# A retention layer and a gated feed-forward on one core: another order of the seven second-layer products, and all first-layer weights through one load queue

## The chip, the core and the metric

The kernel runs on one core of a Trainium2 chip. The metric is the device time of one execution in microseconds (us). Kernels of one experiment call run on the same chip beside the kernel before. Times quoted are medians with the lowest and highest of their runs. A run more than 1.5% above the fastest of its kernel counts as slow, the others as fast. A ratio is the mean time of one kernel's fast runs over the mean of the other's fast runs of the same rounds, so it is not quite the ratio of the medians; its 95% interval follows in brackets. "Faster" or "slower" is said from 2% on.

Five engines work side by side: TensorE (PE in the profile; PEld are its weight loads), VectorE (DVE), ScalarE (ACT), GpSimd (POOL) and SyncE (SP), which here only starts loads and stores. PSUM is the memory that TensorE writes, in banks; SBUF is the working memory.

## The reference, cut to what matters

```python
scores = (q @ k^T) / 8                         # 8 batches x 8 heads, 576 positions, 64 columns
ret = scores * Dmat                            # gamma_h ** (i - j) for j <= i, else 0
x = (ret @ v) as 4608 tokens x 512
h = x @ w_in                                   # 512 -> 2048, the "first layer"
out = (h * cos(h)) @ w_out                     # 2048 -> 512, the "second layer"
```

## The kernel before

The retention is done chunk by chunk with a carried state. I call one chunk's group of small matmuls a *session*: it reads scaled and transposed Q and K tiles and scaled V, masks on VectorE, and leaves output (`xt`) that ScalarE copies for the first layer. The first layer works in *units* of four 128x512 matmuls (or eight of 256 columns): TensorE writes a PSUM bank, ScalarE makes the cosine (`cb`), VectorE multiplies bank and cosine into `gt` (0.69 us each), and only then is the bank free. W_in comes in eight *slabs* of 256 hidden units, float32 in memory, bfloat16 for TensorE.

The second layer of all blocks of 512 tokens but the first uses a seven-product scheme. Each product has two halves of eight 128x256 matmuls (0.87 us). What a product reads decides when it can start:

```python
left = {1: lambda: ((self.S1, HF * HB, 0, HB), [("s1", f) for f in range(HF)]),
        2: lambda: ((self.S5, HF * TB, HB, TB), s5), 3: lambda: of_gt(0, 0), 4: lambda: of_gt(1, 1),
        5: lambda: ((self.S5, HF * TB, 0, TB), s5), 6: lambda: of_gt(0, 1), 7: lambda: of_gt(1, 0)}
```

`of_gt(0, .)` is the lower half of the hidden units, `of_gt(1, .)` the upper half, `S5` and `S1` are sums of `gt` tiles made on VectorE (the *token sums*, four rounds for each block). The order and what follows each product:

```python
seq = ((4, "e", True, p4), (2, "e", False, p2), (3, "f", True, p3), (5, "f", False, p5),
       (1, "a", True, p1), (7, "a", False, p7), (6, "b", True, p6))
if last:
    seq = tuple(seq[i] for i in (0, 2, 4, 1, 3, 5))
```

and their weaving with the next block's units, in which `run` also spreads the sessions evenly:

```python
fs = [f for u in range(HF) for f in (u, u + HF)]        # units 0, 8, 1, 9, ...
for i, f in enumerate(fs[:0 if last else None]):
    ...                                                 # one first-layer unit
    mlp += two[i:i + 1]                                 # one half of a product
    if i in AT:
        mlp.append(lambda u=AT.index(i), j=j: self.token_sums(j + 1, u))
run(mlp, att_of(need[j + 1], need[j + 2]) if j + 2 < NTB else [])
```

This weaving is only the order in which work is handed to a scheduler inside the kernel's builder. It simulates the engines with estimated costs and decides the final order on each engine.

## Time and profile before

| | before |
|---|---|
| three runs before the prediction | 304.32, 304.94, 749.91 us |
| span of the profiled execution | 301.2 us |
| TensorE busy, granted clock | 95%, full speed in every slice |
| session that reads the third V tile (V2) starts | 39.05 us |
| from there to the start of the last matmul | 259.32 us |
| from there to the end | 2.79 us |

The page gives busy shares, the chain that ended last and groups of instructions. A timeline line is: start in us, length in us, engine, source line, operation, output<-input tiles, tile shapes, type, count, and in brackets the idle time before the group with what ended it. The shown end of a matmul lies about 0.17 us after the moment at which the next may start. I measured waits as the distance between the starts of neighbouring matmuls minus the usual distance of such a pair. Where records were missing I lined the trace up with the program's order and took their time out.

### The profile page before, as it was taken

Reading aid. Unit: us, or ns where it says so; the run is one execution under the profiler, and the core shown is the slowest. Engines: PE = TensorE matmul, PEld = TensorE weight load, DVE = VectorE, ACT = ScalarE, POOL = GpSimd, SP = SyncE. Lnnn points to the kernel's source line nnn. Section 1 sums busy time; section 2 is a strip of 40 time slices with the busy share of each in tenths; the row PEclk is TensorE's granted clock in tenths of the full one; section 3 lists DMA queues with packets and bytes.
Section 4 is the critical chain, followed back from the end, with each engine's and each line's share of the span. In section 5 each row is a group of like instructions: output and inputs, shape, how many; then the busy total and the mean of one; then the engine's idle time right before and its main releaser. Section 6 shows DMA issues by size and latency. Waiting matters only on the chain.

```text
span 301.2 us, 8764 instructions
## 1 busy us (share of the span) xinstructions
PE 286.9 (95%) x3637; PEld 204.0 (68%) x3673; DVE 241.0 (80%) x403; ACT 185.8 (62%) x320; POOL 145.1 (48%) x145
## 2 busy tenths in 40 slices
PE   8988999999999999998999899999999999999996
PEld 3467578865788885666667576666666667566585
DVE  5888999999898599789767976898689568847941
ACT  4076567846676567765776568766777676545421
POOL 4715762688555687279217930993140013003213
PEclk9999999999999999999999999999999999999999
DMA  8999999999999999999899946996302020211114
GB/s 205 301 288 278 247 198 217 195 241 215 160 250 227 191 258 226 201 192 193 182 219 226 196 98 155 234 205 143 92 33 74 1 66 6 72 35 37 35 37 139
DMA packets 124438, 49.45 MB, mean 164 GB/s; under 512 B 83952, under 2 KB 123888, under 8 KB 124400
## 3 DMA queue, kind: packets, MB, share of 16 engines
q1 hardware_dynamic: 121232, 45.76, 71.6%
q0 software_dynamic: 3168, 3.15, 6.4%
q8 instruction: 29, 0.48, 0.7%
q14 instruction: 9, 0.07, 0.1%
HBM read 36.70 MB, written 9.44 MB: 153 GB/s over the span
## 4 chain that ended last, share of the span: by engine, by line
PE 78%; DVE 10%; DMA 4%; issue 4%; SPq 3%; ACT 1%; DVEq 0%
PE bk L807 35%; PE bk L924 30%; PE bk L832 5%; DMA stg<-in_v_dram 4%; DVE gt L818 4%; PE st L638 2%; PE bk L617 1%; DVE gt L893 1%; PE bk L608 1%; SPq L424 1%; DVE os L959 1%; PE bk L627 1%; DVE nat L485 1%; SPq L457 1%; DVE s L886 1%
## 5 line engine op out<-in xcount | busy, mean ns | idle before, releaser
L807 PE MATMUL bk<-xt,win 128*128 128x512 bf16 (+2 forms) x781 | 135.5, 316 | 4.3 <-DVE gt L818 1.0
L815 ACT ACTIVATE cb<-bk,cpi 128x512 bf16<-128x512 f32 x144 | 98.4, 687 | 57.9 <-PE bk L807 53.6
L818 DVE TENSOR_TENSOR gt<-bk,cb 128x512 bf16<-128x512 f32 x144 | 97.5, 686 | 38.6 <-ACT cb L815 33.7
L807 PEld LDWEIGHTS bk<-xt,win 128*128 128x128 bf16 x808 | 72.1, 98 | 38.4 <-ACT xt L674 1.3
L959 POOL TENSOR_TENSOR sv<-sv,os 128x512 f32<-128x512 f32 x16 | 22.3, 1391 | 81.7 <-ACT os L968 43.1
L530 POOL TENSOR_TENSOR qnat<-qstg,wt 128x512 bf16<-128x512 f32 x36 | 39.9, 1128 | 17.1 <-DMA qstg<-in_q_dram 17.1
L674 ACT ACTIVATE sbd<-st 64x512 bf16<-64x512 f32 (+1 forms) x68 | 38.0, 559 | 12.6 <-PE bk L608 11.0
L674 ACT ACTIVATE xt<-bk 128x256 bf16<-128x256 f32 (+1 forms) x64 | 27.6, 489 | 19.1 <-PE bk L727 15.1
L520 POOL TENSOR_TENSOR nat<-stg,wt 128x512 bf16<-128x512 f32 x28 | 36.0, 1285 | 5.0 <-DMA stg<-in_v_dram 4.9
L924 PE MATMUL bk<-wout,gt 128*128 128x256 bf16 x256 | 31.6, 273 | 3.0 <-DVE gt L818 3.0
L485 POOL CAST nat<-stg 128x512 bf16<-128x512 f32 x36 | 26.6, 747 | 13.5 <-DMA stg<-in_k_dram 13.5
L924 PE MATMUL bk<-tw,gt 128*128 128x256 bf16 x256 | 32.6, 273 | 0.0
L924 PE MATMUL bk<-wout,s 128*128 128x256 bf16 x256 | 31.8, 273 | 0.0
L924 PEld LDWEIGHTS bk<-wout,gt 128*128 128x128 bf16 x256 | 24.2, 98 | 10.9 <-DVE gt L818 5.8
L886 DVE TENSOR_TENSOR s<-gt 128x1024 bf16<-128x1024 bf16 x32 | 28.3, 904 | 3.1 <-PE bk L924 3.0
L924 PEld LDWEIGHTS bk<-tw,gt 128*128 128x128 bf16 x256 | 24.5, 98 | 7.4 <-ACT sv L963 0.6
L893 DVE TENSOR_TENSOR gt<-gt 128x1024 bf16<-128x1024 bf16 x32 | 29.1, 910 | 0.0
L924 PEld LDWEIGHTS bk<-wout,s 128*128 128x128 bf16 x256 | 24.3, 98 | 6.6 <-DVE gt L818 0.4
L959 POOL TENSOR_TENSOR sv<-sv 128x512 f32<-128x512 f32 x8 | 10.8, 1355 | 23.1 <-ACT sv L963 20.1
L653 DVE TENSOR_TENSOR pt<-bk,tri 128x512 bf16<-128x512 f32 (+3 forms) x37 | 20.3, 565 | 1.5 <-PE bk L608 1.3
L890 DVE TENSOR_TENSOR s<-gt 128x512 bf16<-128x512 bf16 x32 | 18.6, 582 | 0.1
L959 DVE TENSOR_TENSOR os<-bk,sv 128x512 f32<-128x512 f32 (+1 forms) x17 | 10.8, 647 | 7.0 <-POOL sv L959 6.6
(72 smaller groups left out, 258.6 us busy)
## 6 DMA issues: line engine op xcount, KB each, us to landing
out_dram<-os SPq DMA_DIRECT2D x31, 256.0 KB, 3.5
qstg<-in_q_dram SPq DMA_DIRECT2D x12, 512.0 KB, 5.8
stg<-in_k_dram SPq DMA_DIRECT2D x24, 256.0 KB, 4.3
stg<-in_v_dram SPq DMA_DIRECT2D x24, 256.0 KB, 5.1
stg<-in_k_dram SPq DMA_DIRECT2D x4, 512.0 KB, 8.9
stg<-in_v_dram SPq DMA_DIRECT2D x4, 512.0 KB, 9.3
wout<-in_moe_w_out_dram POOLq DMA_DIRECT2D x4, 512.0 KB, 12.5
qstg<-in_q_dram SPq DMA_DIRECT2D x4, 384.0 KB, 7.0
```

The costliest lines, as they stand in the source:

```text
L485: self.P.add(eng, lambda e: e.tensor_copy(dst, src), r=r, w=w, cost=cost, port=eng == "pool")
L520: self.P.add(eng, lambda e: e.tensor_tensor(ap(self.NAT[na], 2 * DM, 0, 128, DM, [D, H], [1, D]), ap(self.STG[st], 2 * DM, 0, 128, DM, [D, ...
L530: self.P.add(eng, lambda e, x=x: e.tensor_tensor(ap(self.QNAT[slot], 2 * DM, 0, 128, x * DM, [D, H], [1, D]), ap(self.QSTG[slot], 2 * DM, ...
L653: inst = e.tensor_tensor(ap(pt, 1024, p0, n, 256 * x, [256, m], [64, 4], [1, 64]), ap(self.BK, NB * 512, p0, n, (lo, hi)[x] * 512 + 256, [ ...
L674: self.P.add(eng, (lambda e: e.activation(*io(), AF.Copy)) if eng == "act" else (lambda e: e.tensor_copy(*io())), r=r, w=w, cost=0.127 + 0 ...
L807: inst = e.matmul(self.bk(box.i, 0, 128, i * n, n), ap(self.WIN, 4 * DFF, 0, 128, c * DFF + 128 * f, [1, 128]), ap(self.XT, 4 * XR, 0, 128 ...
L815: self.P.add("act", lambda e: e.activation(ap(cb, TB, 0, 128, 0, [1, m]), self.bk(box.i, 0, 128, 0, m), AF.Sin, bias=self.CPI.ap(), scale= ...
L818: self.P.add("dve", lambda e: e.tensor_tensor(ap(gt, NF * TB, 0, 128, f0 * TB + lo - TB * j, [TB, len(fs)], [1, n]), self.half_bank(box.i, ...
L886: self.P.add("dve", lambda e: e.tensor_tensor(ap(self.S5, HF * TB, 0, 128, f * TB, [1, 2 * TB]), ap(gt, NF * TB, 0, 128, f * TB, [1, 2 * TB]),
L893: self.P.add("dve", lambda e: e.tensor_tensor(ap(gt, NF * TB, 0, 128, f * TB + HB, [HF * TB - HB, 2], [TB, 2], [1, HB]), ap(gt, NF * TB, 0 ...
L924: inst = e.matmul(self.bk(box.i, 0, 128, at * HB, HB), ap(lt, lsize, 0, 128, loff + f * lstep + 128 * t, [1, 128]), ap(rt, rsize, 0, 128, ...
L959: self.P.add(eng, lambda e: e.tensor_tensor(out(), a(), b(), op), r=r, w=w, cost=1.04 if eng == "pool" else 0.09 + 0.00104 * n * HB, port= ...
```

## The change

The intent is threefold: get the V tiles sooner by putting all slabs on one queue behind K2; take the wait before each block's first product away by starting with product 3, which reads only lower units that are ready early when units run in rising order; and hold the last product back so that TensorE has something to do behind the last unit.

```diff
-AT = (9, 10, 12, 15)
+HOLD = (2, 4)
+LS = (0, 1, 2, 3, 4, 5)
+AT = (9, 11, 13, 15)
-EO, ES, EQ = ('act', 'act'), ('dve', 'act'), ('pool', 'pool')
-WP = (5, 5, 6, 8, 7, 8, 10, 1)
-WC = ("dve", "act", "act", "dve", "pool", "dve", "act", "dve")
-G1, G2, WG = 5, 5, ("stg", 1, 1, 0)
-EARLY = 8
-SOFT = (2, 6)
+EO, ES, EQ = ('act', 'act'), ('dve', 'dve'), ('pool', 'dve')
+WP = (7, 7, 7, 7, 8, 7, 7, 10)
+WC = ("dve", "act", "act", "dve", "pool", "dve", "dve", "act")
+G1, G2, WG = 3, 5, ("stg", 1, 1, 0)
+EARLY = 12
+SOFT = ()
-SHIFT = ('dve', 'dve')
-UNITS = ((0, 256, (0, 10)), (256, 512, (0, 10)), (0, 512, (10, 16)))
+SHIFT = ('act', 'dve')
+UNITS = ((0, 256, (0, 12)), (256, 512, (0, 12)), (0, 512, (12, 16)))
...
-        seq = ((4, "e", True, p4), (2, "e", False, p2), (3, "f", True, p3), (5, "f", False, p5),
+        seq = ((3, "f", True, p3), (4, "e", True, p4), (2, "e", False, p2), (5, "f", False, p5),
                (1, "a", True, p1), (7, "a", False, p7), (6, "b", True, p6))
         if last:
-            seq = tuple(seq[i] for i in (0, 2, 4, 1, 3, 5))
+            seq = tuple(seq[i] for i in LS)
...
-        BYPE, LEAD = 13, 2
+        BYPE, LEAD = 14, 2
...  (two cost estimates of the scheduler: a slab load 1.45 to 1.55, a product 0.9% more)
...  (K transposes copied by ScalarE instead of VectorE, in two places)
-                    self.step_tk(t, "dve")
+                    self.step_tk(t, "act")
...
-            for i, f in enumerate(fs[:0 if last else None]):
+            for f in range(0 if last else NF):
...
-                mlp += two[i:i + 1]
-                if i in AT:
+                mlp += two[f:min(f + 1, 14 - HOLD[j + 2 == NTB])]
+                if f in AT:
...
+            mlp += two[14 - HOLD[j + 2 == NTB]:14 if not last else 0]
```

`SOFT = (2, 6)` sent slabs 2, 3, 6 and 7 by two loads of GpSimd's queue that wrote bfloat16 directly; without it all eight slabs are cast by an engine. `BYPE` is the first group whose Q and K are turned by DMA instead of TensorE. I call the constants of the first group together with the K copies and `BYPE` the *start part*, the rest the *boundary part*.

More of the change, by code (lines that the diff above doesn't have):

```diff
@@ L459, in load_win @@
             bass.AP(self.w_in, s * 256, [[DFF, 128], [128 * DFF, 4], [1, 256]])),
-            w=keys, sem=f"wi{s}", cost=0.62, ring=1.45, pkt=0.04)
+            w=keys, sem=f"wi{s}", cost=0.62, ring=1.55, pkt=0.04)
     def load_soft(self, s, gate):
@@ L929, in mm @@
             return inst
-        self.P.add("pe", mm, r=lk + rk, w=[box], cost=HF * HB * 0.000422)
+        self.P.add("pe", mm, r=lk + rk, w=[box], cost=HF * HB * 0.000427)
     def bank(self, box, n=2):
@@ L976, in summed, with p3, p4 @@
             self.store(TB * j + HB * h + 128 * t, n, HB * c, HB, o)
-        def p4():
-            save("e", 0)
+        def p3():
+            save("f", 0)
         def p2():
             plain("e", 1, 0)
-        def p3():
-            add("dve", lambda: sv[0], lambda: self.bank(box["f"]), lambda: sv[0], ALU.add,
-                [box["f"], ("sv", 0)], [("sv", 0)])
+        def p4():
+            add("dve", lambda: sv[0], lambda: self.bank(box["e"]), lambda: sv[0], ALU.add,
+                [box["e"], ("sv", 0)], [("sv", 0)])
         def p5():
@@ L1119, in schedule @@
             for t in self.twos(tiles[g]):
-                self.step_tk(t, "dve")
+                self.step_tk(t, "act")
             for k in quads[g]:
@@ L1137, in schedule @@
         run([m1(lo, hi, *fs) for lo, hi, fs in units[EARLY:]], [lambda: T(need[0])] + att_of(need[0], req(640)))
-        fs = [f for u in range(HF) for f in (u, u + HF)]
         sums = [x for y in zip(self.weight_sums(0), self.weight_sums(1)) for x in y]
@@ L1151, in schedule @@
             mlp = two if last else []
-            for i, f in enumerate(fs[:0 if last else None]):
+            for f in range(0 if last else NF):
                 if j > 1:
                     mlp.append(m1(TB * (j + 1), TB * (j + 2), f))
-                elif i % 2 == 0:
-                    mlp.append(m1(1280, 1536, *(f // 2 * 2 + i % 4 // 2 * HF + x for x in range(2))))
-                mlp += two[i:i + 1]
-                if i in AT:
-                    mlp.append(lambda u=AT.index(i), j=j: self.token_sums(j + 1, u))
+                elif f % 2 == 0:
+                    mlp.append(m1(1280, 1536, f, f + 1))
+                mlp += two[f:min(f + 1, 14 - HOLD[j + 2 == NTB])]
+                if f in AT:
+                    mlp.append(lambda u=AT.index(f), j=j: self.token_sums(j + 1, u))
+            mlp += two[14 - HOLD[j + 2 == NTB]:14 if not last else 0]
             run(mlp, att_of(need[j + 1], need[j + 2]) if j + 2 < NTB else [])
```

## The prediction

> **What bounds the kernel now.** I read the busy summary and the forty slices first, then the TensorE timeline for every idle stretch, then the chain of waits for the start and the timeline for the tail.
>
> ```profile
> PE 286.9 (95%) x3637; PEld 204.0 (68%) x3673; DVE 241.0 (80%) x403; ACT 185.8 (62%) x320; POOL 145.1 (48%) x145
> ...
> PE   8988999999999999998999899999999999999996
> ...
> PEclk9999999999999999999999999999999999999999
> ```
>
> TensorE (PE) is busy nearly everywhere at the full clock. I check that by its pace, because the shown end of a matmul lies about 0.17 us behind the moment at which the next can start (four 128x512 matmuls are shown as 1.03 us long, yet the next group starts 0.87 us later). A first-layer unit (four 128x512 matmuls) takes 0.864 us of pace, half a second-layer product (eight 128x256) 0.87 us. That makes 144 units x 0.864 = 124.4, 112 halves x 0.87 = 97.4 and 64 plain second-layer matmuls x 0.216 = 13.8, together 235.6 us. None of it changes. So time can only come from TensorE's waits, from the start before it has steady work, and from the tail.
>
> ```profile
> 37.35 1.02 PE L807 MATMUL bk<-xt,win 128*128 128x512 bf16 x4 [0.46 <-DVE gt L818]
> 39.05 0.44 PE L721 MATMUL st<-sv,nat 64*64 64x64 bf16 x16 [0.68 <-DVE pt L698]
> ...
> 113.57 2.54 PE L807 MATMUL bk<-xt,win 128*128 128x512 bf16 x11 [0.55 <-ACT xt L674]
> ...
> 139.89 1.92 PE L924 MATMUL bk<-wout,gt 128*128 128x256 bf16 x16 [0.69 <-DVE gt L818]
> ...
> 170.71 1.92 PE L924 MATMUL bk<-wout,gt 128*128 128x256 bf16 x16 [1.23 <-DVE gt L818]
> ...
> 200.64 1.05 PE L924 MATMUL bk<-wout,gt 128*128 128x256 bf16 x8 [0.39 <-DVE gt L818]
> ...
> 286.25 3.67 PE L924 MATMUL bk<-wout,gt 128*128 128x256 bf16 x32 [0.71 <-DVE gt L818]
> ```
>
> The bracket is the idle time before the group and what ended it. These seven are all the real ones after 26.2 us; the many brackets of 0.16 beside groups of 3 or 11 are matmul records missing from the trace. With the 0.17 us added back they are worth 0.62, 0.84, 0.71, 0.86, 1.39, 0.55 and 0.88 us, 5.85 us in all. The last four are one event: a block's first product, number 4, reads the upper hidden units and waits until the last first-layer unit has gone through ScalarE (0.69 us) and VectorE (0.69 us).
>
> ```profile
> 9.34 11.38 DMA stg<-in_v_dram
> 20.74 1.29 DVE sv L509 x2
> 23.52 1.30 DVE gt L818 x2
> 26.30 5.39 PE bk L807 x48
> ```
>
> This is the start of the chain of waits. The second V load is issued at 9.3 us and lands at 20.7, because two W_in slabs on the same queue and two more through GpSimd's queue go before or beside it. TensorE is saturated only from 26.2 us.
>
> **What the Trainium skill says.** "Perfetto Trace Analysis", section Identifying the Most-Contended Engine, says that matmul busy share is a poor measure because matmuls are pipelined; the trace agrees (1.03 us shown, 0.87 us of pace), hence the count by pace. "DMA: Bandwidth & Descriptors", section Issuing engines are not separate DMA queues, says that DMAs started by different engines interleave on the same 16 DMA engines. The trace agrees: from 12.14 to 20.72 us two slabs (1.51 us each), one V load (1.8 us) and a 1 MB load of GpSimd's queue land, the last taking the remaining 3.8 us. So moving those slabs to the other queue makes no bandwidth; it only lets me choose the order. "SBUF — State Buffer", section Who interferes with whom, says that a VectorE instruction with two SBUF inputs contends with a GpSimd one that reads SBUF. The trace fits: the token sums (128x1024) average 904 ns, and 0.68 us at the end where GpSimd is idle.
>
> **The change, part by part.**
>
> *Start, worth about -1.85 us.* All eight slabs now go through the sync queue, behind K0 Q0 V0 K1 Q1 V1 K2. With the measured paces in the trace (K, Q or V 1.8 us, slab 1.51 us, Q1 at 12.14) I get: V1 13.95 (was 20.72), K2 15.75 (22.54), slab 0 17.3 (13.65), slabs 1, 2, 3, 5, 6 at 18.8, 20.3, 21.8, 23.3, 24.8, Q2 26.6 (25.82), slab 4 28.1, V2 29.9 (31.65), K3 31.7, slab 7 33.2, Q3 35.0, V3 36.8 (37.65). The bytes are the same, so the end of the loads hardly moves; V comes sooner, the first slab later.
> I then followed the order of instructions in the built program with durations from the trace. VectorE paces the stretch from 14 to 25 us: it has half of the Q scaling (0.7 us), V scaling 2 x 0.69, state copies 2 x 0.41, the Q transpose's copy 0.69, slab 0's cast 0.68, four masks 2.5 us. First first-layer unit: 19.95 us (was 17.6). Third big session: its mask at 21.1. Slab 1, cast on ScalarE (1.06 us) and then a table load (1.28 us), feeds the second unit at 21.95; slab 2's cast ends at 22.95 and feeds the third. Fourth session from about 23.95, then the steady stream from about 25.0 with three 256-column units done, against 26.24 with four: 1.24 - 0.87 = 0.37 us gained. From there the transpose copies (13 x 0.41 us) and half of the shifts (8 x 0.36 us) are off VectorE, which was 96 to 100% busy from 30 to 70 us, so I expect the two waits at 37.35 and 39.05 to go: 1.46 us. The session that started at 39.05 should start at about 37.2; equal TensorE work lies before it in both programs.
>
> *Block boundaries, -3.7 us.* Product 3 reads only the lower hidden units, early in the rising order, and its 1.75 us cover the last unit's way through ScalarE and VectorE before product 4. Two halves of product 6 (1.74 us) are held back behind the last unit as well. Three boundary waits go: 0.86 + 1.39 + 0.55. The 0.71 at 113.57 (a session's output was not yet copied) goes too, since the built program has five halves of products (4.4 us) after that session instead of two; with some 0.2 us of small waits near 177 to 200 us that is 3.7.
>
> *Last block, about 0.* The 0.88 at 286.25 goes by the same means (four halves held, 3.5 us). But the order is now 3, 4, 2, ..., and product 2 needs all token sums. Between the last unit's end and product 2 TensorE has 3.5 + 3.5 = 7.0 us of work. VectorE has about 1.7 us until that unit's output, then two output sums (2 x 0.68), two full rounds of token sums (2 x 1.74) and two of the third (1.06): 7.6, partly waiting for products. I expect a new wait of 0.9 us there, which eats the gain.
>
> *Tail, +0.45 us.*
>
> ```profile
> 295.86 1.27 POOL L959 TENSOR_TENSOR sv<-sv,os 128x512 f32<-128x512 f32 x1 [0.41 <-ACT os L968]
> 297.22 1.02 DVE L959 TENSOR_TENSOR os<-bk,sv 128x512 f32<-128x512 f32 x2 [6.58 <-POOL sv L959]
> ...
> 298.68 0.42 DVE L959 TENSOR_TENSOR os<-bk,sv 128x256 f32<-128x256 f32 x1 [0.44 <-PE bk L924]
> ```
>
> The GpSimd chain of the last block ends 1.5 us before TensorE does. Product 1 moves from third to fifth place, so its save (0.6) and two GpSimd sums (2 x 1.27) start only 3.5 us before TensorE's end and finish at about that end; then come two VectorE sums (2 x 0.42) where one came before.
>
> *Elsewhere, +1.2 us.* One more K and one more Q tile are transposed on TensorE (4 + 8 matmuls of 56 ns): +0.67. For new small waits I allow 0.5, since product 3's PSUM bank is now held across products 4 and 2.
>
> Sum: -1.85 - 3.7 + 0 + 0.45 + 1.2 = -3.9 us.
>
> **Rivals.**
> (a) The start gives more. If VectorE's queue does not hold up the first units (slab 0 is there at 17.3), the stream starts up to 2.5 us sooner: about 298 us. Against it: every VectorE item of that stretch stands in program order before slab 0's cast.
> (b) The start gives nothing or loses. W_in now arrives later than V; if a slab is late (slab 4, behind Q2 and cast by GpSimd, or slab 7), TensorE stalls between 29 and 36 us for 1 to 2 us: about 302.5. For it: my slack at slab 4 is only 2 us.
> (c) PSUM banks become the bound. Products 3/5 and 4/2 hold two of six banks together where one was held, and a session needs two. A wait of 0.4 us in each of seven blocks would take 2.8 us back: about 303. Against it: with products between them, units come only every 1.74 us and hold a bank about 2.7 us.
> (d) The gain is hidden by something already there, such as the loads. Against it: DMA is under 40% busy from 210 us on, and TensorE sets the pace.
>
> **Range and chances.** The two good runs before were 304.32 and 304.94; from 304.5, 3.9 less is 300.6. Block boundaries are the surest part (2.8 to 4), the start the least sure (+1 to -4), the tail within half a microsecond. A gain above 2% needs 6.1 us, more than all listed waits (5.85): only rival (a) together with full success elsewhere gives it. Slower by 2% would need several new waits at once. So 298.0 to 303.4, with 0.16, 0.82, 0.02.
>
> **What would show it right or wrong.** V1 landing near 14 us and slab 0 near 17.3; first unit near 20, stream from about 25; the big session that reads V2 starting near 37.2 without a wait; no wait on a hidden-unit product (VectorE line of the first layer) before a block's first product; a wait of about 1 us before product 2 in the last block; two 128x256 output sums on VectorE after TensorE's last matmul. It would be wrong if TensorE shows new waits for ScalarE or VectorE in the middle of blocks, or a wait for slab casts around 30 us, and wrong in the other direction if the stream starts before 23 us.

## The result and the profile after

Four runs each on one chip: after 302.55 us (301.96 to 302.69), before 307.41 us (304.32 to 749.91), ratio of the fast runs 0.9928 [0.9900, 0.9956]. Later the same kernel after gave 302.72 (301.91 to 304.72) against 304.02 (302.99 to 309.01), ratio 0.9979 [0.9945, 1.0012]. So the change is worth 0.2 to 0.7%, some 0.6 to 2.2 us: the same within 2%, and in the second, whose interval includes 1, not clear of the noise. The forecast change was 3.9 us.

The busy lines of the page of the kernel after:

```profile
PE 288.0 (96%) x3659; PEld 206.2 (69%) x3695; DVE 239.5 (80%) x384; ACT 197.7 (66%) x340; POOL 143.7 (48%) x141
...
PE   8879899999999999999899999999999999999995
```

The shares hardly differ from before. ScalarE has 20 instructions and 12 us more, VectorE 19 instructions and only 1.5 us less: the moved K and V copies took 7.5 us off VectorE, and slab casts (2.1 us), state copies (1.7), Q scaling (1.4) and longer token sums (2.6 in the 128x512 ones) filled most of it.

TensorE's timeline of the kernel after at the start:

```profile
20.44 1.05 PE L809 MATMUL bk<-xt,win 128*128 128x256 bf16 x8 [0.42 <-DVE win L487]
...
24.33 1.05 PE L809 MATMUL bk<-xt,win 128*128 128x256 bf16 x8 [0.59 <-ACT win L484]
...
26.25 0.94 PE L809 MATMUL bk<-xt,win 128*128 128x256 bf16 x7
```

The steady stream starts at 26.25 us, as before (26.24), but with 24 of the small first-layer matmuls done instead of 32. Eight times 0.109 us is 0.87 us of deficit. The third unit waited for slab 2's cast on ScalarE.

TensorE's timeline of the kernel after further on, at the places of the waits:

```profile
37.02 0.40 PE L695 MATMUL bk<-qt,kt 64*128 64x128 bf16 x8 [0.57 <-DVE qt L541]
37.84 2.14 PE L809 MATMUL bk<-xt,win 128*128 128x512 bf16 x8 [0.41 <-DVE gt L820]
39.91 0.44 PE L723 MATMUL st<-sv,nat 64*64 64x64 bf16 x16
...
147.00 0.39 PE L619 MATMUL bk<-qt,sbd 128*128 128x64 bf16 x8 [0.57 <-issue]
...
209.50 1.05 PE L926 MATMUL bk<-wout,s 128*128 128x256 bf16 x8 [0.29 <-DVE s L888]
...
285.36 3.66 PE L926 MATMUL bk<-wout,gt 128*128 128x256 bf16 x32
288.85 3.33 PE L926 MATMUL bk<-wout,s 128*128 128x256 bf16 x29
```

The two waits near 38 us did not go (0.74 and 0.58 us, and 0.25 inside the group of eight). The four waits of `wout,gt` products behind the last unit are gone, the one of 0.88 at the last block among them: the held products reach to 285.36, products 3 and 4 from there to 288.85, and product 2 follows, all without a bracket. New are 0.74 us at 147.00 and 0.46 at 209.50.

VectorE's timeline of the kernel before, and then of the kernel after, in front of V2's session:

```profile
35.19 1.29 DVE L485 COPY nat<-sv 64x512 bf16<-64x512 bf16 x2
36.51 1.29 DVE L818 TENSOR_TENSOR gt<-bk,cb 128x512 bf16<-128x512 f32 x2
37.72 1.28 DVE L698 TENSOR_TENSOR pt<-bk,trb 128x512 bf16<-128x512 f32 x2
```

```profile
34.95 1.30 DVE L487 COPY nat<-sv 64x512 bf16<-64x512 bf16 x2
36.27 0.69 DVE L541 COPY qt<-bk 128x1024 bf16<-128x1024 bf16 x1
37.00 0.69 DVE L820 TENSOR_TENSOR gt<-bk,cb 128x512 bf16<-128x512 f32 x1
37.61 1.28 DVE L700 TENSOR_TENSOR pt<-bk,trb 128x512 bf16<-128x512 f32 x2
```

In both kernels the masks (`pt`) end at 38.9 to 39.0 us, with VectorE busy without a gap from the V copies on. V2 had landed at 31.65 and 31.55 us, and GpSimd had scaled it by 33.96 and 33.73.

The tail of the kernel after, in the timeline of all engines:

```profile
296.31 1.27 POOL L961 TENSOR_TENSOR sv<-sv,os 128x512 f32<-128x512 f32 x1
...
296.91 1.46 DVE L961 TENSOR_TENSOR os<-bk,sv 128x512 f32<-128x512 f32 x3 [6.57 <-PE bk L926]
```

GpSimd's last sum now ends at 297.58, just about with TensorE's last matmul (started 297.48), and VectorE has its three sums in one run behind it. Tail 3.35 us instead of 2.79.

The ledger of the two profiled executions: V2's session 39.05 to 39.91 (+0.86), from there to the last matmul 259.32 to 257.57 (-1.75), tail +0.56, sum -0.33, which is the difference of the spans (301.16 and 300.83). The profiled execution of before was one of its faster ones (303.02 us with the launch), so the usual difference is about a microsecond more.

### The profile page after: what moved, and what is told of

It reads as the page before. It is cut to its first block, busy times and chain, and to the rows that moved or that the text cites.

```text
span 300.8 us, 8802 instructions
## 1 busy us (share of the span) xinstructions
PE 288.0 (96%) x3659; PEld 206.2 (69%) x3695; DVE 239.5 (80%) x384; ACT 197.7 (66%) x340; POOL 143.7 (48%) x141
## 4 chain that ended last, share of the span: by engine, by line
PE 80%; ACT 5%; DVE 4%; SPq 4%; DMA 3%; issue 2%; POOLq 0%; POOL 0%; DVEq 0%
PE bk L809 37%; PE bk L926 31%; PE bk L834 4%; DMA gt<-in_moe_w_in_dram 3%; ACT cb L817 2%; SPq L426 2%; PE st L640 2%; PE bk L619 2%; DVE gt L820 2%; PE bk L610 1%; PE bk L629 1%; SPq L445 1%; PE bk L567 1%; ACT xt L676 1%; ACT win L484 1%
## 5 line engine op out<-in xcount | busy, mean ns | idle before, releaser
L809 PE MATMUL bk<-xt,win 128*128 128x512 bf16 (+2 forms) x788 | 133.7, 314 | 4.2 <-DVE gt L820 1.0
L820 DVE TENSOR_TENSOR gt<-bk,cb 128x512 bf16<-128x512 f32 x144 | 95.9, 685 | 37.4 <-ACT cb L817 36.1
L961 POOL TENSOR_TENSOR sv<-sv,os 128x512 f32<-128x512 f32 x16 | 21.0, 1315 | 87.9 <-ACT os L970 66.7
L532 POOL TENSOR_TENSOR qnat<-qstg,wt 128x512 bf16<-128x512 f32 x34 | 38.9, 1164 | 19.2 <-DMA qstg<-in_q_dram 18.2
L676 ACT ACTIVATE sbd<-st 64x512 bf16<-64x512 f32 (+1 forms) x64 | 36.5, 570 | 15.0 <-PE bk L610 13.6
L926 PE MATMUL bk<-tw,gt 128*128 128x256 bf16 x256 | 31.3, 273 | 0.0
L655 DVE TENSOR_TENSOR pt<-bk,tri 128x512 bf16<-128x512 f32 (+2 forms) x30 | 19.8, 663 | 3.8 <-PE bk L610 3.7
L892 DVE TENSOR_TENSOR s<-gt 128x512 bf16<-128x512 bf16 x32 | 21.3, 664 | 0.0
L961 POOL TENSOR_TENSOR sv<-sv 128x512 f32<-128x512 f32 x8 | 13.2, 1656 | 15.5 <-ACT sv L965 10.3
L970 ACT ACTIVATE os<-bk 128x512 f32<-128x512 f32 x16 | 9.6, 597 | 13.0 <-PE bk L926 12.9
```

Of the source, the lines that this page charges most:

```text
L532: self.P.add(eng, lambda e, x=x: e.tensor_tensor(ap(self.QNAT[slot], 2 * DM, 0, 128, x * DM, [D, H], [1, D]), ap(self.QSTG[slot], 2 * DM, ...
L676: self.P.add(eng, (lambda e: e.activation(*io(), AF.Copy)) if eng == "act" else (lambda e: e.tensor_copy(*io())), r=r, w=w, cost=0.127 + 0 ...
L809: inst = e.matmul(self.bk(box.i, 0, 128, i * n, n), ap(self.WIN, 4 * DFF, 0, 128, c * DFF + 128 * f, [1, 128]), ap(self.XT, 4 * XR, 0, 128 ...
L820: self.P.add("dve", lambda e: e.tensor_tensor(ap(gt, NF * TB, 0, 128, f0 * TB + lo - TB * j, [TB, len(fs)], [1, n]), self.half_bank(box.i, ...
L892: self.P.add("dve", lambda e: e.tensor_tensor(ap(self.S1, HF * HB, 0, 128, f * HB, [HB, 2], [1, HB]), half(0, 0), half(1, 1), ALU.add), r= ...
L926: inst = e.matmul(self.bk(box.i, 0, 128, at * HB, HB), ap(lt, lsize, 0, 128, loff + f * lstep + 128 * t, [1, 128]), ap(rt, rsize, 0, 128, ...
```

## The experiments

All eighteen runs had five rounds (six times each, eleven of before). "V2" is the start of V2's session. "Waits" is the sum of TensorE's waits over 0.1 us after 55 us. Comparisons across calls are rough: the interval of again alone is 0.0067 wide, 2 us. Where two kernels differ by less than a microsecond, the argument rests on their traces and not on their times.

| run | median (lowest to highest) | before in the call | ratio of fast runs | V2 | waits |
|---|---|---|---|---|---|
| again | 302.72 (301.91-304.72) | 304.02 | 0.9979 [0.9945, 1.0012] | 39.7 | 2.4 |
| bound_only | 304.35 (302.23-308.15) | 304.02 | 1.0003 [0.9971, 1.0035] | slow profile | |
| start_only | 304.74 (304.31-306.20) | 304.02 | 1.0044 [1.0019, 1.0069] | 39.9 | 5.5 |
| no_extra_transposes | 303.69 (303.43-304.45) | 304.02 | 1.0003 [0.9984, 1.0022] | 39.9 | 3.3 |
| bound_only_2 | 303.67 (303.44-309.73) | 303.70 | 1.0002 [0.9985, 1.0019] | 39.5 | 4.1 |
| shift_act | 305.81 (305.61-305.89) | 303.70 | 1.0070 [1.0056, 1.0084] | 39.9 | 3.4 |
| last_1_third | 301.85 (301.60-302.06) | 303.70 | 0.9940 [0.9927, 0.9953] | 39.6 | 1.7 |
| no_hold | 303.66 (303.53-304.38) | 303.70 | 1.0004 [0.9989, 1.0019] | 40.0 | 3.7 |
| bound_bype14 | 303.86 (302.29-309.43) | 304.15 | 0.9987 [0.9957, 1.0016] | 38.9 | 2.7 |
| bound_bype14_third | 302.89 (302.24-303.66) | 304.15 | 0.9963 [0.9942, 0.9985] | 38.8 | 2.3 |
| at_before | wrong result | 304.15 | not used | | |
| bound_loads | 305.80 (305.33-305.99) | 304.15 | 1.0057 [1.0038, 1.0076] | 41.0 | |
| last_1_third_2 | 302.18 (301.77-303.40) | 304.31 | 0.9950 [0.9926, 0.9975] | 39.6 | |
| slabs_sooner | 306.18 (305.45-306.80) | 304.31 | 1.0074 [1.0053, 1.0095] | 41.4 | 3.2 |
| slab4_dve | 303.14 (301.93-303.91) | 304.31 | 0.9975 [0.9951, 0.9998] | 40.4 | |
| slabs_sooner_slab4 | 306.21 (305.15-307.39) | 304.31 | 1.0076 [1.0049, 1.0103] | 41.6 | |
| slabs_0_1_7_sooner | 303.38 (302.95-303.91) | 304.51 | 0.9959 [0.9913, 1.0005] | 40.0 | |
| slab7_sooner | 303.93 (303.01-304.68) | 304.51 | 0.9975 [0.9931, 1.0018] | 40.5 | |

For before the sum of waits is 4.7 us, for after 2.0.

### The change in two parts

**again** is the kernel after, unchanged.

> The changed kernel once more, for a tighter time. Both theories: 0.990 to 0.996 of the kernel before, fourth-pair session (the one that reads V2) again starting at 39.5 to 40.3 us of the trace.

The session came when expected (39.7 us), the ratio did not: 0.9979 lies above the 0.990 to 0.996.

**bound_only** keeps the boundary part and gives the start part back to before (the constants from `EO` to `UNITS`, `BYPE = 13`, K copies on VectorE, two cost estimates). **start_only** is the opposite.

```diff
 # bound_only, against after
-        BYPE, LEAD = 14, 2
+        BYPE, LEAD = 13, 2
-                    self.step_tk(t, "act")
+                    self.step_tk(t, "dve")
 ...  (EO to UNITS as in before)
 # start_only, against before: the same lines the other way round
```

> The kernel before with only the block part of the change (order 3, 4, 2, 5, 1, 7, 6, rising f, two or four halves held, token sums after units 9, 11, 13, 15). Theory A (the start of the changed kernel loses, the boundaries gain): it is the faster half, 2.5 to 3.5 us below the kernel before (ratio 0.988 to 0.992), session of V2 near 39.05 us as before, no wait at block boundaries. Theory B (the new product order makes waits of its own, the start is neutral): only 1 to 2 us below (0.993 to 0.997), with new waits in the middle of blocks.

> The kernel before with only the start part (all W_in slabs on the sync queue behind K2, half of Q scaling on VectorE, K transposes copied by ScalarE, half of the shifts by ScalarE, one more session transposed on TensorE), old product order. Theory A: slower than the kernel before by 1 to 2 us (1.003 to 1.007), V2's session near 39.9 us. Theory B: equal within 0.5 us (0.998 to 1.002).

The profile of bound_only fell in the slow state (its run was over 1.5% above the fastest of the same kernel), so I ran it again as bound_only_2:

> The same kernel as bound_only, whose profile fell in the slow state: new product order, rising units and held-back products with the start of before. Theory A (the boundary part is a real gain of 2.5 to 3.5 us and the start costs 1): a fast profile shows the session of V2 starting near 39.05 us as in before, none of the waits 0.86, 1.39, 0.55, 0.71 and 0.88 of before, and less than 1.5 us of new waits in their place; time 301.5 to 302.5, ratio 0.990 to 0.995. Theory B (the new order makes as many waits as it removes): new waits of 2.5 us or more between 100 and 290 us, ratio 0.998 to 1.003. Theory C (the first 40 us are unstable: VectorE's copies of the V tiles collide with GpSimd): the waits near 37 to 42 us differ by over 1 us between this profile and that of bound_only, and the rounds spread over more than 3 us.

Theory C held for the slow execution. A line of TensorE's and one of VectorE's timeline of bound_only, and then VectorE's of bound_only_2:

```profile
40.39 1.02 PE L809 MATMUL bk<-xt,win 128*128 128x512 bf16 x4 [2.73 <-DVE gt L820]
...
36.60 2.92 DVE L487 COPY nat<-sv 64x512 bf16<-64x512 bf16 x2
```

```profile
35.74 1.16 DVE L487 COPY nat<-sv 64x512 bf16<-64x512 bf16 x2
```

In the slow execution these two V copies took 1.87 and 1.02 us (0.42 and 0.71 in bound_only_2), beside GpSimd's issuing of the W_out loads and its K casts (34.08 to 38.28). TensorE waited 2.90 us for VectorE where bound_only_2 waits 0.49, and from 42.51 us its granted clock was 0.5 for 3.41 us. The profile of slabs_sooner has such a stretch too, at 41.40 us, behind waits of 1.33 and 1.84 us; no other profile has one before its last matmul. One stretch brings the mean over 304 us down to 0.994, about what this run lists (0.993), so the 0.989 and 0.983 that other slow runs list would be two and three of them: an estimate, since none of those was profiled. Of the 55 executions of before in the five calls, 16 took over 307 us, all with a clock of 0.983 to 0.994; so did 3 of the 24 of other kernels with its start, and none of the 46 of after, last_1_third (both calls), no_hold, no_extra_transposes, start_only and shift_act, which have the new start. That late copies are behind all of these is likely, but one profile shows it, and no run tests what made them late.

The parts don't add. The boundary part on the old start is worth nothing (1.0003 and 1.0002), the start part on the old order costs 1.3 us (1.0044), and both together gain. Put differently, the boundary part took start_only's 304.74 to 302.72, 2.0 us, and took before's 304.02 nowhere. This contradicts theory A as I had written it, and theory B only fits one of the two starts. TensorE's timeline of start_only:

```profile
144.08 1.05 PE L924 MATMUL bk<-wout,gt 128*128 128x256 bf16 x8 [0.93 <-DVE gt L818]
...
174.13 1.05 PE L924 MATMUL bk<-wout,gt 128*128 128x256 bf16 x8 [0.34 <-DVE gt L818]
...
203.89 1.05 PE L924 MATMUL bk<-wout,gt 128*128 128x256 bf16 x8 [0.42 <-DVE gt L818]
...
289.54 1.70 PE L924 MATMUL bk<-wout,gt 128*128 128x256 bf16 x14 [0.77 <-DVE gt L818]
```

These are before's four waits for the last unit, at 3.1 us together (with the 0.17 each). In after they are gone. Most of the rest of start_only's 5.5 us are waits of 0.48, 1.27 and 0.40 us between 113 and 125 us. TensorE's timeline of bound_only_2 shows what comes in their place on the old start:

```profile
115.04 3.63 PE L809 MATMUL bk<-xt,win 128*128 128x512 bf16 x16 [1.48 <-ACT xt L676]
119.33 0.39 PE L619 MATMUL bk<-qt,sbd 128*128 128x64 bf16 x8 [0.66 <-issue]
...
122.39 1.81 PE L926 MATMUL bk<-wout,s 128*128 128x256 bf16 x15 [0.34 <-DVE s L888]
```

A session began at 110.80, only two halves of a product (1.74 us) followed it, and then a unit had to read that session's output, which ScalarE finished copying at 115.0. The three waits are 3.0 us. In after the session stands at 108.89 us with five halves of products behind it, and of these waits 0.28 us is left.

### What moves the session

**no_extra_transposes** is after with one edit.

```diff
-        BYPE, LEAD = 14, 2
+        BYPE, LEAD = 13, 2
```

> The changed kernel with one session less transposed on TensorE (13 in place of 14, as before). My reckoning of 12 matmuls of 56 ns: 0.7 us faster than the changed kernel. Rival: nothing, or slower, because the DMA transposes of that session then come in late beside the loads and TensorE waits for them.

The tile on TensorE costs 12 transposes, 0.67 us, yet taking it off made the kernel no faster, rather 0.7 us (by the ratios) to 1.0 us (by the medians) slower than again, at the edge of the noise: waits of 0.43, 0.59, 0.66 and 0.53 us came back between 114 and 127 us. So its main effect isn't its cost but where the scheduler puts the sessions. Is that all that bound_only lacked? **bound_bype14** gives bound_only this one line, **bound_bype14_third** also the tail edit below.

```diff
 # bound_bype14, against bound_only
-        BYPE, LEAD = 13, 2
+        BYPE, LEAD = 14, 2
```

> The kernel bound_only (order, rising units and held products of after, with the start of before) and one thing more: tile 13 is transposed on TensorE, as after does, not by DMA. In after and in bound_only_2 the sessions stand at different places among the products, though the order of the products is the same, because the tile adds 12 matmuls to the stream; bound_only_2 waits 1.64, 0.82 and 0.50 us at 115, 119 and 122 us, after waits only 0.28 there. Theory D (the gain of the boundary part hangs on where the sessions fall, and the extra tile shifts them): those three waits shrink to under 1 us together, and with the start of before the time is 0.9 us under after, 301.6 to 302.1, ratio 0.992 to 0.995. Rival (the extra tile only costs its 0.67 us, and the start of after is what makes the gain): time 303.7 to 304.5, ratio over 1.000.

> The same with product 1 third in the last block, which brought last_1_third 0.7 to 0.9 us. If the parts add up: 0.5 to 0.9 us under bound_bype14, so 301.0 to 301.5, the fastest of all, ratio 0.990. Rival: in last_1_third only 0.17 us of the difference was the tail itself and the rest a smaller wait near 147 us that has nothing to do with product 1; then 0.2 us under bound_bype14 at most.

Half of theory D held, and the time is the rival's (303.7 to 304.5). The waits from 115 to 126 us fell from 3.0 to 1.2 us, and V2's session started 0.8 to 0.9 us sooner than in again, which is the price of the new start seen in after. But the time didn't fall to 302: the profile shows 1.23 instead of 0.48 us at 37.2, 1.06 at 46.4 (not in the profile of bound_bype14_third, whose program is the same there) and two of 0.5 us at 168.8 and 209.9. The two kernels differ by 0.7 us in their fast means, the size that last_1_third had promised, but with this start the fast runs of one kernel alone spread over 2 us, and the tail of bound_bype14_third is not shorter but longer (3.59 us against 3.35).

**no_hold** is after without held products.

```diff
-HOLD = (2, 4)
+HOLD = (0, 0)
```

> The kernel after, with no products held behind the last unit. Theory 1 (product 3 in front alone covers the last unit's way through ScalarE and VectorE, 1.4 us against its 1.75): the boundary waits stay under 0.3 us each, and the wait near 147 us gets smaller, since three units no longer follow each other with so little between: time as after or 0.5 better. Theory 2 (holding is what removes the waits): waits of 0.3 to 0.9 us before product 4 come back at five boundaries, time 1.5 to 3 us over after.

Neither theory's number. It costs some 0.8 us against again (0.0025 in the ratio), most of it in two waits of product 4, 1.40 us at 177.53 and 0.73 at 207.42. At the other boundaries product 3 alone was enough, and the wait at 147 us was gone. Holding matters in some blocks only, and again through where things fall.

**at_before** put the token sums of after behind units 9, 10, 12 and 15.

```diff
-AT = (9, 11, 13, 15)
+AT = (9, 10, 12, 15)
```

> The kernel after with the four rounds of token sums behind units 9, 10, 12 and 15, as before had them, instead of 9, 11, 13 and 15. In after VectorE is in these sums from 141.3 to 146.2 us, the output of a first-layer unit waits behind them, its PSUM bank comes free late, and TensorE's session stops 0.74 us (1.59 in the repeat) at 147. If the sums' place makes that wait: it changes by 0.5 us or more (gone if the sums end sooner), and so does the 0.45 at 209.5 before the product that reads the sums; time 0.5 us under after. Rival (VectorE has that much to do in any order, the wait comes from three units in a row): the two waits together stay within 0.4 us of 1.2 to 2.4 us, time as after within 0.4.

My mistake: the result was wrong (relative error 0.58) and the time says nothing. Round u of the sums reads units 2u, 2u+1, 2u+8 and 2u+9, so with rising units round 1 may not come before unit 11, and I had let it read at unit 10. That is why the change moved `AT`. A build with (10, 12, 14, 15) had the same order on every engine as (9, 11, 13, 15): the scheduler places the sums by itself.

### The wait near 147 us

No experiment isolates this wait, but executions of programs that are the same up to the last block differ there. In again it is 1.59 us. VectorE's timeline of again:

```profile
142.27 1.53 DVE L888 TENSOR_TENSOR s<-gt 128x1024 bf16<-128x1024 bf16 x1
143.72 1.26 DVE L892 TENSOR_TENSOR s<-gt 128x512 bf16<-128x512 bf16 x1
...
146.10 1.87 DVE L820 TENSOR_TENSOR gt<-bk,cb 128x512 bf16<-128x512 f32 x3
```

GpSimd's timeline of again at that time:

```profile
140.75 2.49 POOL L532 TENSOR_TENSOR qnat<-qstg,wt 128x512 bf16<-128x512 f32 x2 [1.85 <-DMA qstg<-in_q_dram]
143.21 1.49 POOL L522 TENSOR_TENSOR nat<-stg,wt 128x512 bf16<-128x512 f32 x1
```

And VectorE's timeline of last_1_third, where GpSimd did the same work 1.4 us sooner and was done at 142.6:

```profile
143.09 0.68 DVE L888 TENSOR_TENSOR s<-gt 128x1024 bf16<-128x1024 bf16 x1
143.69 0.41 DVE L892 TENSOR_TENSOR s<-gt 128x512 bf16<-128x512 bf16 x1
```

The same two sums took 2.79 us beside GpSimd and 1.09 alone. In after and last_1_third_2 they took 1.93 and 1.94 us, and the wait was 0.74 and 0.88: longer sums, longer wait, in all four executions. In again a unit whose cosine was ready at 143.58 was multiplied only at 146.10, so its PSUM bank stayed taken, and TensorE's session, which needs banks, began at 146.88, 0.1 us after that multiplication ended. In last_1_third the wait there is 0.20 us, with another of 0.59 at 142.76. The Trainium skill's "SBUF — State Buffer", section Who interferes with whom, says that a VectorE instruction with two SBUF inputs contends with a GpSimd instruction that reads SBUF; these durations agree. So the "issue" in after's line is best read as rival (c) of the prediction, banks held by VectorE's queue, though a run that only frees VectorE there is missing.

### The tail

**last_1_third** puts product 1 back to third place in the last block.

```diff
-LS = (0, 1, 2, 3, 4, 5)
+LS = (0, 1, 4, 2, 3, 5)
```

> The kernel after, with product 1 third in the last block (3, 4, 1, 2, 5, 7 without 6), as the kernel before had it. If the tail's extra 0.56 us comes from product 1's place (GpSimd's sums then end behind TensorE): last TensorE start to the end 2.8 us instead of 3.35, time 0.5 us under after, ratio to after 0.998. Rival: product 1, which needs token sums of its own, comes before they are done, and TensorE waits 0.5 to 1 us before it, which eats the gain: time as after within 0.3.

> A repeat of last_1_third as the base of this call. If its gain over after is real (the tail and nothing else differs in the program): 301.6 to 302.2 again, ratio 0.993 to 0.996. If part of it was luck at 143 to 147 us, where its profile showed waits of 0.59 and 0.20 against 0.74 in after and 1.59 in the repeat, though the program is the same there: 302.2 to 302.7, and the profile shows another pair of waits there.

Both came in below after: 301.85 and 302.18, ratios 0.9940 and 0.9950; the mean of the twelve runs is 302.1 against 302.8 of after's ten. No wait appears before product 1. But the tail only fell from 3.35 to 3.18 us in both profiles, not to 2.8. The repeat's waits at 147 and 209 us are after's (0.88 and 0.47), so the first profile's smaller one at 147 (0.20, with 0.59 at 142.76) is no merit of the edit. Its span was 300.5, after's two were 300.8 and 301.0: about 0.4 us is the edit, of which 0.17 is the tail as I defined it. The rest I can't assign. It is the fastest kernel, ahead of both, though within 2% like all the others.

### The start

**shift_act** moves VectorE's V copy to ScalarE.

```diff
-SHIFT = ('act', 'dve')
+SHIFT = ('act', 'act')
```

> The kernel after, with both shift copies of a V tile on ScalarE instead of one on VectorE. Theory C (VectorE's 64x512 copies at 34.95 us were stretched to 1.30 us by GpSimd's work and held up the query scaling behind them): the waits of 0.74 and 0.57 us at 37.0 and 37.8 us shrink to under 0.4 together, the V2 session starts near 38.9 instead of 39.9, time 1 us under after (301.7), and the rounds spread less. Rival: these copies then stand in ScalarE's queue behind the slab casts and cosines, the first-layer units come later and the waits only change their releaser: V2's session still at 39.7 to 40.2, time as after or up to 1 us worse.

The rival was right and too mild: 3.1 us slower than again. V2's session stayed at 39.9, the wait before it is now one of 1.68 us for ScalarE's cast of the last slab, and 0.74 and 1.11 us for ScalarE's copies follow at 47.7 and 49.1. ScalarE has no room there.

**bound_loads** is bound_bype14 with the loads, slab casts and first units of after (`WP`, `WC`, `G1`, `EARLY`, `SOFT`, `UNITS`), but without its moved copies.

> The kernel bound_bype14 with the loads of after (all slabs through the sync queue behind K2, slab casts and first-unit order of after), but the copies, shifts and evictions of the start where before has them. If the late slabs are what the start of after loses (slab 1 lands at 20.25, slab 2's cast on ScalarE ends at 24.3): steady stream with the 0.9 us deficit, V2's session at 39.9 or later, time 0.5 to 1.5 us over bound_bype14. Rival (the moved copies and shifts lose it, by the VectorE copies that GpSimd stretches to 1.3 us at 35 us): V2's session at 39.3 or sooner, time as bound_bype14 or better.

1.9 us slower than bound_bype14, V2's session at 41.0. So the loads lose at the start, together with the slab casts and the order of units that go with them. But they don't lose in the way that I expected: slab 1 landed at 18.82 us here, not at 20.25, and V2 at 30.82, sooner than in after (31.55). The step from here to after is the moved copies and evictions (and the two cost estimates of the scheduler): V2's session at 39.7 to 39.9, and a ratio of 0.9979 instead of 1.0057 (another call, so roughly 2.4 us). Those copies more than pay for the loads that they came with. Then three kernels on the base of last_1_third asked which load:

```diff
 # slabs_sooner: slabs 0 and 1 ahead of K2
-WP = (7, 7, 7, 7, 8, 7, 7, 10)
+WP = (6, 6, 7, 7, 8, 7, 7, 10)
 # slab4_dve: slab 4 cast by VectorE instead of GpSimd
-WC = ("dve", "act", "act", "dve", "pool", "dve", "dve", "act")
+WC = ("dve", "act", "act", "dve", "dve", "dve", "dve", "act")
 # slabs_sooner_slab4: both
```

> last_1_third with slabs 0 and 1 ahead of K2 in the sync queue instead of behind it. Theory S (slab 1's late landing delays ScalarE's cast, its table load and slab 2's cast): slab 1 lands near 18.5 instead of 20.25, slab 2's cast ends near 22.9 instead of 24.3, the steady stream has one unit more done at 26.2, V2's session starts near 38.8 instead of 39.6, time 0.6 to 0.9 us under last_1_third. Rival V (VectorE's chain sets the pace until 39 us): the first units come sooner but V2's session still starts at 39.3 to 40, the waits before it grow, time within 0.4 us of last_1_third.

> last_1_third with slab 4's cast on VectorE instead of GpSimd, where it stands between Q2's and V2's scaling. Theory G (GpSimd's chain is what V2 waits for): V2's scaling ends near 32.7 instead of 33.7, the V2 copies start 0.7 to 1 us sooner, the waits of 0.71, 0.58 and 0.25 us at 36.7 to 38.7 shrink by 0.7 or more together, time 0.5 to 0.9 us under last_1_third. Rival V: VectorE has 0.7 us more to do, and the same waits stand there or come sooner; time as last_1_third or up to 0.7 us over.

> Both edits. If both theories hold they add up to 1.2 to 1.6 us under last_1_third (300.3 to 300.6), the best of all; if VectorE's chain is the limit, within 0.5 us of last_1_third; if each reshuffle of the start only moves the later sessions to other places, anything from 0.5 under to 2 us over, with new waits of 0.5 us or more between 100 and 210 us.

TensorE's timeline of slabs_sooner:

```profile
25.16 1.52 PE L809 MATMUL bk<-xt,win 128*128 128x256 bf16 x12
...
37.01 1.90 PE L809 MATMUL bk<-xt,win 128*128 128x512 bf16 x8 [1.16 <-ACT win L484]
...
40.91 0.40 PE L695 MATMUL bk<-qt,kt 64*128 64x128 bf16 x8 [1.67 <-DVE gt L820]
```

Theory S was right about its own step: slab 1 landed at 17.16, slab 2's cast ended at 22.84, and the stream began at 25.16 with the same 24 matmuls done, 1.1 us sooner than in after. Yet the kernel lost 4 us, in the profiled execution partly to the halved clock behind the waits. TensorE ran out of units at 37.0, waiting 1.33 us for slab 7's cast (landed 34.73, cast until 36.96), then 1.84 us for VectorE. slab4_dve gained nothing either: a unit waited 0.91 us for that cast at 33.28 and another 0.93 us for slab 7 at 38.58. Together they came out as slabs_sooner alone.

So the last slab came into view. Before, it landed complete at 30.3 us and needed no cast; after, it is ready at 36.94. Two kernels brought it forward, ahead of K3:

```diff
 # slabs_0_1_7_sooner, against last_1_third
-WP = (7, 7, 7, 7, 8, 7, 7, 10)
+WP = (6, 6, 7, 7, 8, 7, 7, 9)
 # slab7_sooner, against last_1_third
-WP = (7, 7, 7, 7, 8, 7, 7, 10)
+WP = (7, 7, 7, 7, 8, 7, 7, 9)
```

> slabs_sooner and also slab 7 ahead of K3 in the sync queue. Theory L (the last slab takes the gain): slab 7 lands near 33.1, its cast ends 1.5 us sooner, the wait of 1.3 us at 37.0 goes and with it most of the 1.8 at 40.9, V2's session starts at 38.8 to 39.6, time 302 to 303.5 against 306.2. Rival V (VectorE's and GpSimd's chain behind V2's landing at 31.5): the wait only moves to another releaser, V2's session at 40.8 or later, time 305 or more.

> last_1_third with slab 7 alone ahead of K3. In last_1_third no wait before V2's session is for slab 7 (they are 0.71, 0.58 and 0.25 us, all for VectorE), so with either theory the waits stay: V2's session at 39.3 to 39.9, time within 0.5 us of last_1_third plus what the reshuffled sessions make of it (up to 1.5 us over). A time over 0.5 us below last_1_third would mean that ScalarE's cast at 35.9 to 36.9 us held up the cosines there.

Slab 7 was then cast by 35.10, and slabs_0_1_7_sooner ran in 303.38 instead of 306.18: about 3 us were the last slab's. But V2's session only came to 40.0, and its TensorE timeline has the wait at the very same place, with another name:

```profile
37.01 1.04 PE L809 MATMUL bk<-xt,win 128*128 128x512 bf16 x4 [1.16 <-ACT kt L540]
...
39.10 0.81 PE L809 MATMUL bk<-xt,win 128*128 128x512 bf16 x3 [0.73 <-ACT cb L817]
```

slab7_sooner alone was no gain: 0.8 us (by the ratios) to 1.8 us (by the medians) over last_1_third, as the reshuffling allowed for, with V2's session at 40.5, later than I had expected. Nothing that I did to the loads brought V2's session before 39.6 in a kernel with the new start.

## Why the prediction was right or wrong

**Direction and total.** The time landed inside the range (302.55 for 298.0 to 303.4), but the gain was 0.6 to 2.2 us instead of 3.9, and 0.3 between the two profiled executions. That it fell on rival (b)'s 302.5 is luck: the stall for a late slab between 29 and 36 us, from which that rival had its number, did not come in after. The terms of the sum, from the two profiles:

| term | forecast | measured |
|---|---|---|
| start (V2's session) | -1.85 | +0.86 |
| block boundaries and last block | -3.7 + 0 | -4.4 |
| extra transposes and new waits | +1.2 | +2.7 |
| tail | +0.45 | +0.56 |
| sum | -3.9 | -0.3 |

**The start is the step that failed, by 2.7 us.** Its two halves were "0.37 us gained" for the stream and "I expect the two waits at 37.35 and 39.05 to go: 1.46 us". Measured, the stream lost 0.87 us, and 1.57 us of waits (0.74, 0.58, 0.25) stood before V2's session. Against before that is 0.87 us more work still to do and 0.11 us more waiting, which gives the 0.86 within 0.12.

- Slab 1 landed at 20.25, not 18.8. V1 (14.06), K2 (15.85) and slab 0 (17.35) had kept to my times. ScalarE cast slab 1 from 20.27, loaded its cosine table from 21.34 to 22.62, made one cosine, and cast slab 2 until 24.27: the third unit's wait. The Trainium skill's "ScalarE: Activation LUTs", section What ACT_TABLE_LOAD costs, has 1283 ns for that load, and the trace 1.28 us. slabs_sooner supports that this landing held up the stream: with slab 1 at 17.16 it began 1.1 us sooner. It isn't the only thing that can: in bound_loads slab 1 landed at 18.82, as forecast, and the stream began at 26.51 with only 16 small matmuls done, the first of them held until 23.72 by a copy of ScalarE.
- I had taken "equal TensorE work lies before it in both programs" to mean that V2's session moves with the stream. The work is equal, but the session also needs V2, which I had forecast at 29.9 and which landed at 31.55, as before. GpSimd's scaling to 33.7 and VectorE's unbroken run to 38.9 follow in both kernels. Before began the session right behind that run, at 39.05; after, with its deficit, had one more unit to do first (38.94 to 39.91). An earlier stream alone did not help either: slabs_sooner and slabs_0_1_7_sooner began it 0.8 us sooner than last_1_third and reached V2's session 0.4 to 1.8 us later.
- VectorE was not relieved where it counts. I took the moved copies off its account after 25 us and did not set the extra slab casts against them (two more on VectorE, two more on ScalarE than before). Rival (b) named late slabs (4 or 7). In after only slab 2 held up a unit; slab 7 does so at 37 to 38.6 us in the variants, as soon as anything before it gets faster.

That V2's path is the floor is suggested by the equal times in both traces, but a sooner V2 was not enough in bound_loads: it landed at 30.82 there, VectorE's V copies were done at 35.17 (36.24 in after), and the masks still began only at 39.65. How the time up to V2's session divides between TensorE's deficit, V2's path and the queues of VectorE and ScalarE stays open.

**Block boundaries: right, and the last block better than forecast.** All five waits of 113.57, 139.89, 170.71, 200.64 and 286.25 are gone in after, 4.4 us. The "new wait of 0.9 us" before product 2 in the last block did not come: I had charged VectorE with 7.6 us against TensorE's 7.0, but product 2 followed without a bracket. In no_hold, where nothing is held, 0.38 us of it shows.

But the reason that I gave for the wait at 113.57, "five halves of products after that session instead of two", I had put to the product order. bound_only_2 and no_extra_transposes have the new order and wait there 0.4 to 1.6 us all the same. It is the extra tile's shift of the sessions that clears it, a thing that I had booked as pure cost.

**Elsewhere: mis-sized by 1.5 us.** The transposes are 0.67 us as forecast. For new waits I allowed 0.5; after has 0.66 us at 41 to 49 us and 2.0 us later (0.38 at 59, 0.28 at 118, 0.74 at 147, 0.46 at 209 and smaller ones), while pauses under 0.1 us became some 0.7 us fewer. Rival (c) was the one to watch: not "0.4 us in each of seven blocks" but 0.7 to 1.6 in the one where GpSimd's scaling meets the token sums.

**Tail: right within 0.11 us, its mechanism only half.** VectorE's end moved from 0.73 to 0.89 us after the last matmul's start. The other 0.4 us of the 0.56 lies in issuing and landing the last store, which the prediction did not have.

## What to carry to other kernels

Before crediting an earlier start, follow everything that the next fixed point needs (here TensorE's own work, the third V tile and VectorE's queue) and check that all of it moves; otherwise the gain is waited away. Where a scheduler places work, a small edit has two prices, its own instructions and the places that it gives to everything else; the second was larger here (0.7 against over 1 us), so test parts together as well as alone. A wait removed from a tightly packed engine counts only when the sum of its waits has fallen: here from 4.7 to 2.0 us with both parts, but to 4.1 with the boundary part alone and to 5.5 with the start part alone.

## What the Trainium skill lacked or had wrong

- "ScalarE: Activation LUTs", section What ACT_TABLE_LOAD costs: it adds a drain of about 1380 ns to each switch, 2.66 us in all. In after the cast before the load ends at 21.32, the load runs from 21.34 to 22.62 and the first cosine starts at 22.64: 1.32 us in all, no drain to be seen.
- "SBUF — State Buffer", section Who interferes with whom, has no length for a VectorE copy beside GpSimd's issuing of loads: in after a 64x512 bfloat16 copy took 0.28 us at 18.3 and 0.55 and 0.71 us at 35, while GpSimd was issuing the W_out loads (33.67 to 36.87), and in the slow execution of bound_only 1.87 and 1.02 us. That one caused the other was not tested.
- "Runtime: NRT & Kernel Launch" has no figure for what the fetch of instructions costs the loads beside it, and no page that I read names it as a cost of loads. In every profile where all slabs go through the sync queue, one load was late: slab 1 in after came 2.90 us after slab 0 (1.5 elsewhere), K2 in slabs_sooner 3.03 us after slab 1 (1.8 elsewhere). The packets of after's trace show one of 16 KB in the queue that the profile page lists as instruction (q8), from 17.57 to 18.73 us, just then. In bound_loads, with the same order of loads, it came from 19.59 to 20.65, and there slab 1 took its 1.50 us and slab 2, which landed at 21.00, took 2.18. That the packet holds up the load is likely, not tested: the next one in after, at 27.17, made no single load late by more than 0.2 us.
